# Another recorded order of steps and other engine choices for the first part of an attention and Fourier-mixing kernel

## The chip, the cores and the metric

The kernel runs on one core of a Trainium2 chip. A core has TensorE (PE, matrix products, 128x128 cells that can also work as smaller tiles), VectorE (DVE), ScalarE (ACT) and GpSimd (POOL), each with its own instruction queue that is worked off in order, and SyncE (SP), from whose queue nearly all DMAs of this kernel are issued. The metric is the device time of one execution in microseconds (us).

## The reference

Everything is float32; the two weights of the last step come as float64. 8 batches, 8 heads, a sequence of 576, heads of 64.

```
attention, for each batch and head, q and k scaled by 64**-0.25:
  phi(t) = exp(h - max(h)) / sqrt(128),  h = t @ omega.T - sum(t*t)/2      # 128 features
  kv = phi(k).T @ v;  z = sum of phi(k) over the sequence
  out = (phi(q) @ kv) / (phi(q) @ z + 1e-6)
x = heads side by side                       # (8, 576, 512)
u  = x + real(fft over features(fft over sequence(x)))
un = (u - mean(u)) / sqrt(var(u) + 1e-6)
result = u + relu(un @ w_ch1) @ w_ch2        # w_ch1 512x2048, w_ch2 2048x512
```

## The kernel before, in words

The program has two parts. Both are written as streams: Python generators that yield a `Step` ahead of each small group of instructions. A step names the engine (or a choice of engines with a cost for each), what it waits for, which buffers and PSUM banks it takes and gives back, and, for TensorE, the tile mode. `Listing.run` (L194) goes through the streams, decides whose step comes next and, where there is a choice, on which engine, and so writes each engine's queue. What runs when on the chip is then set by these queues and by semaphores.

**First part** (to about 422 us). Lanes `pairs(0)`, `pairs(1)`, `pairs(2)` go through 32 pairs of heads; `attn(n)` (L585) is one pair:

- `loads` brings k (L388) and q (L391), `load_v` v (L396); TensorE transposes (L524, identity as the other operand) and `evicted` copies the result out as kqT on VectorE (L538) or ScalarE (L540).
- Features: L618 in 64x128 tiles for the first six pairs and 64x64 tiles after; VectorE takes the maximum (L561), ScalarE the exponential (L578).
- kv: L652 in 64x64 tiles, copied out at L666 (VectorE) or L668 (ScalarE). Exponentials of q are transposed by L524 again and copied to qeT.
- Numerator and denominator: L699 and L707 in 128x64 tiles; reciprocal on VectorE (L716, L717), quotient on VectorE (L728) or ScalarE (L724).

`mix(b)` (L740) is the Fourier step of a batch: folds (L755, L757, L761, L771, L784) on VectorE or GpSimd, products with tables of cosines and sines (L811 in whole 128x128 tiles and L821), copies (L834), a second set of products (L861, L872), sums, and stores of u. At the very start `warm` (L495) has six matmuls on zeros that depend on no load, and `first` (L503) transposes omega (tile om).

Woven in: `narrow` (L439) turns float64 weights into float32 in several passes, the first on ScalarE (L451) or GpSimd (L449), the others on VectorE, the last sum (L467) on either; `w2_parts` (L1273) and `weight_sums` (L1352) form sums of weight blocks; and four blocks of 128 tokens go through both layers of the MLP plainly (`plain_of`: L1127 with relu at L1111 on VectorE or L1113 on ScalarE, then L1150). Each float32 matmul stands in the profile as two records.

In this part the choices are recorded in the string `PICKS`, one character for each step. Its value, divided by 36, gives the position of the stream in the list of those that wait, as remainder, and `other` as quotient: 0 takes the engine that by the planner's clock would be done first, 1 the next. `FIRST` holds the constants of that clock; `turn` is what a change of tile mode costs TensorE in it; VectorE and GpSimd share one time `PORT`, up to which operations on the shared port wait in the plan.

**Second part** (from about 422 us). The other 3584 tokens go through the MLP in seven blocks of 512, by a scheme of Strassen's kind with fewer products and more sums. L1454 and L1596 are first-layer products, L1839 second-layer ones; sums are made by `add` (L1414, recorded as L1419) on VectorE or GpSimd, the result of products by L1477, L1497, L1401 (VectorE), L1479, L1511, L1577, L1812 (ScalarE) and others. `wash` (L1944) clears three PSUM banks behind a GpSimd memset (L1948). `w1_sums` (L1653) builds sums of weight blocks into tiles so5, so6 and so3, `w1_inner` (L1681) sums within them into tile rx. Here nothing is recorded: the planner decides on the go, with the clock `SECOND`, from the state in which the first part leaves its engines:

```
    listing.run([wash(), late_turns(), late_norms(), halves(), load_leaves(), token_sums(0), w1_sums(), w1_inner()])
```

Of the kernel before, what the change touches and what calls it, by code (L numbers as in the profile page):

```python
# [32 lines left out]
NL = 2  # L33
# [3 lines left out]
PE, ACT, DVE, POOL, SP, NONE = "pe", "act", "dve", "pool", "sp", "none"  # L37

PORT = "port"

class Clock(NamedTuple):
# [11 lines left out]
    270.0, 0.036, 0.2, 0.12, {PE: 0.163, ACT: 0.105, DVE: 0.085, POOL: 0.02}, {DVE: 0.12, ACT: 0.055},  # L53
# [3 lines left out]
SLACK, AHEAD = 0.3, 4.0  # L57
# [3 lines left out]
DIGITS = "0123456789abcdefghijklmnopqrstuvwxyzABCDEFGHIJKLMNOPQRSTUVWXYZ!#$%&()*+,"  # L61
# [6 lines left out]
    "40e0f03eafdaegebg3NbcbeefdcOdeccfgdb37ghj0gjj7hlP79Kj7ik97i8S7efhjffeHldfPiehdjfdOShgihidaKOdbRhciff"  # L68
    "ecgOfeejdfdPdeeedgSfdffdOfd8Kiii88jhd8jP8b99i8e8jcddghjgheiifcecdciieicgPgdef9cdghbkededfgchbggb79ij"
    "8hi7hjaPN97aj9gfffeg8eif8hcej1jccc7ehidbhffLiQObfbeG766gggfcbjahj9Ofghhjj8dgkkgT6jghff8de6dUjfhbgegh"  # L70
    "MefRafjUf8jgciSjeckkhjakkaeikggjlioklnRSgodonON7l7l6nnj9icadc97cibPJIej788a7edhclhkmjjagVijihkkfpVim"
    "oklilTTillaghlhnmVjkmpjkhhnmkimlgglmbjpjjg9d9alafhhdjlacdTback0j766k7lh4g89Gck6gkki77gij5ijhgj6dimni"
    "3ndjgi6Kc4jldlaikbkaijbhf75dcjlmUVUDGci45jciekajkkUk5kihoUeaeobaiodlenMSdonbiiljjcWjjkboijjkkhgMfkik"
    "hiflkmOFF99nol5m8jT7naabda89Rbj97ecdl8cjilegiPkQb4acahg57ebbgabgdjkdTkk6eceebb5f9dg4RGce486ggg6egfhh"
    "fg4g9egf5cbdRgfhhhcgjhggejigibbmHnbedijj6Neb7biihi9bgihckaffPa8cijdhbdghbaeibdefffacjiciQSfi9JJ75ih5"
    "jgjI699ajfg6g7fgefd65bO6Kalkkgd5jgjikagfldliPJpeoaeeOPQNejadgilgicljiSSFe65k56kl5Hk7j67S9lilk9gliih6"
    "ffUgec4fg4dbgg7fedaif5gfbheefilddddddeQhg9kbfncggRcfkkafkag6ngb65p5Hopoj4bhoaXbelli68bjjl5b7dlhiQRhi"
    "lflhpkgiWomjknmmmUimnjbjhnJjkm5akPFgedccff6Wf7idUVhi8Th3fogbqp8fgmkeidjna7ckeXYghmnmffnjeo79q6547oa4"
    "nlkpd7aceonnc8bViVicilbhmjim8fh7Snn8l5mkkPjgfRhfhihg8ghfbS4kjf83j4lllb79jei8mnUblfnmmiolpilOki9Mh5l5"
    "pmnaOm79jjVmkbblekFiji9a9kffjgjikhiihfgjafhgfigh4g50fff0ba5fdh9dghda77hgfdcbg8eO988jcehefibjjkellPcc"  # L80
    "fcdhgcihPgcffba2f82b3c98cbcdcd6a299efgddb9KGQQbefLa9ecf74gg9867RgP9idg8kgOhePP7be6ff2e5cc8fbMgdaf8f8"
    "9hd9bM999bddc7cdb7ec9effegd7ibhgeQ8hKf7ccghRlUikh7m5lWmm5dkMQ6M71fS6d1gdb99747ifddh8fdhhdhfdbihgiljn"
    "gWgijgQ93ekal8kEhIIbT3jjagkb9k9eTfhkhlje34m49974i666h68fa7e6eHK79982975a894a39M8cM8b4aK7ab984fgO8ebc"
    "J8b86ce8Pb5fc9cbe6caff3a9b94f8dIQe9abd876e9fdcFPdb7ffbf99SS8RiLa4a7gPbajfgg8gdfhg2i2787Hf6OcdIN5d3LH"
    "accd46ddeaa72d9c7bbaa4bb9a9bc7c0777dghhdP7Bfddebd76ff1fddIe9949438686bcGaca8F348dHc67a5be95Hb55d15E4"
    "9Gc1F5a9a6844634458E584E59189970955888574443113301110"
# [39 lines left out]
class Listing:  # L126
# [4 lines left out]
    def __init__(self, buffers):  # L131
        self.clock = FIRST
        self.free = dict.fromkeys((PE, ACT, DVE, POOL, SP, NONE, PORT), 0.0) | self.clock.begin
        self.buffers = {name: [0.0] * n for name, n in buffers.items()}
        self.made = {}
        self.moved = 0.0
        self.mode = "whole"
        self.banks = [0.0] * 8
        self.got = None
        self.front = 0.0  # L140
# [15 lines left out]
    def start(self, step, ready, before, other=False, due=None):  # L156
# [35 lines left out]
        return t + (clock.turn if eng == PE and step.mode != self.mode else 0.0), eng  # L192

    def run(self, streams, picks=None):  # L194
# [16 lines left out]
        for g in streams:  # L211
            due, g = g if isinstance(g, tuple) else (0.0, g)
            go_on([due, g, None, (0.0, 0.0), NONE])
        while todo:
            pick = next(picks, None)
            other, n = divmod(DIGITS.index(pick), 36) if pick else (0, 0)
# [11 lines left out]
            step = item[2]  # L228
# [64 lines left out]
def kernel(  # L293
# [291 lines left out]
    def attn(n):  # L585
# [18 lines left out]
        def pairs_of(js, *ts):  # L604
# [3 lines left out]
                (0.25 if wide else 0.23) * len(js),  # L608
# [52 lines left out]
        def keep():  # L661
# [23 lines left out]
            1.22,  # L685
# [54 lines left out]
    def mix(b):  # L740
# [102 lines left out]
        for c in range(NC3):  # L843
# [3 lines left out]
                1.38 if c < NL else 0.94,  # L847
# [425 lines left out]
    def w2_parts():  # L1273
# [22 lines left out]
        for i, made_of in (  # L1296
# [16 lines left out]
            yield Step(SP, 3.0, 4.0, after=(("w2t", i),), kb=7 * 256, makes=("w2l", i))  # L1313
# [696 lines left out]
```

## Time and profile before

| | |
|---|---|
| median of three executions | 1138.2 us (1138.0 to 1138.83) |
| profiled execution, its own time | 1138.29 us |
| its span | 1136.3 us |
| TensorE busy | 1116.1 us (98%) |
| VectorE busy | 871.9 us (77%) |
| ScalarE busy | 544.6 us (48%) |
| GpSimd busy | 423.5 us (37%) |
| DMA moved | 258.28 MB |
| granted TensorE clock, mean | 0.999 |

An engine's busy time is the sum of its instructions' spans; where it is near the span, the engine is either at work or called so by a model (ends of matmuls are modelled, so starts are the firmer times). The chain that ended last is followed back from the last instruction and tells what it hung on. Windows show how the shares differ in time: the first part is a mixture of all engines, the second mostly products. A wait is idle time just before an instruction, and the arrow behind it names who ended it. L numbers are lines of the kernel.

### The profile page before, as it was taken

The page shows a single profiled execution, that of the slowest core. Times are in us where ns is not written, and L with a number is a line of the kernel's source. Part 1 is how long each engine was busy: PE and PEld are TensorE (multiplying, and loading weights), DVE is VectorE, ACT ScalarE, POOL GpSimd, SP SyncE. Part 2 cuts the span into 40 slices and gives each one's busy share as a digit, 9 for nine tenths or more (in the row PEclk, how much of TensorE's full clock was granted, in tenths as well). Part 3 has the DMA queues.
Part 4 walks back from the last instruction along what each step waited for, and adds up shares of the span by engine and source line. Part 5 has one row for each costly group of instructions (what it writes and reads, how often), then busy time and mean ns, then how long its engine had stood idle before and what let it go on. Part 6 is the DMA issues. An engine that isn't in the chain of part 4 may idle for free.

```text
span 1136.3 us, 34262 instructions
## 1 busy us (share of the span) xinstructions
PE 1116.1 (98%) x13639; PEld 1039.7 (91%) x13640; DVE 871.9 (77%) x1735; ACT 544.6 (48%) x1646; POOL 423.5 (37%) x435
## 2 busy tenths in 40 slices
PE   8999999999999999989999999999999999999998
PEld 7778888879868768989999999999999999999998
DVE  6999899987576646787777678678678678678666
ACT  7898898856535216724424424423523522522311
POOL 2443443553573124512711710720630540550361
PEclk9999999999999999999999999999999999999999
DMA  7856766575663238597797797798698798788576
GB/s 241 229 184 178 225 181 199 176 216 173 206 203 120 84 109 266 184 320 248 220 333 242 212 333 250 205 314 275 199 302 276 222 288 291 216 264 296 185 224 203
DMA packets 187965, 258.28 MB, mean 227 GB/s; under 512 B 52384, under 2 KB 83360, under 8 KB 187808
## 3 DMA queue, kind: packets, MB, share of 16 engines
q1 hardware_dynamic: 187312, 255.85, 72.2%
q8 instruction: 108, 1.77, 0.6%
q14 instruction: 49, 0.40, 0.1%
q10 hardware_dynamic: 496, 0.26, 0.1%
HBM read 212.27 MB, written 47.97 MB: 229 GB/s over the span
## 4 chain that ended last, share of the span: by engine, by line
PE 92%; DVE 2%; DMA 2%; ACT 2%; issue 1%; SPq 0%; POOL 0%; DVEq 0%; POOLq 0%
PE banks L1839 31%; PE banks L1454 27%; PE banks L618 5%; PE banks L1127 5%; PE banks L524 5%; PE banks L1150 4%; PE banks L1596 4%; PE banks L652 3%; PE banks L699 2%; PE banks L861 2%; PE banks L811 1%; DMA kq<-in_q_dram 1%; PE banks L821 1%; PE banks L872 1%; ACT e L578 1%
## 5 line engine op out<-in xcount | busy, mean ns | idle before, releaser
L1839 PE MATMUL banks<-wl,sums 128*128 128x128 f32 x1792 | 219.0, 275 | 3.3 <-issue 3.2
L1839 PEld LDWEIGHTS banks<-wl,sums 128*128 128x128 f32 x1792 | 209.3, 192 | 3.7 <-issue 3.7
L578 ACT ACTIVATE e<-banks,nmx 128x128 f32<-128x128 f32 x576 | 163.9, 421 | 23.0 <-DVE nmx L561 22.5
L1419 POOL TENSOR_TENSOR hid<-hid 128x512 f32<-128x512 f32 x98 | 128.8, 1318 | 118.7 <-ACT hid L1511 66.5
L1839 PE MATMUL banks<-wl,hid 128*128 128x128 f32 x1344 | 170.4, 275 | 0.4 <-DVE part L1817 0.4
L1839 PEld LDWEIGHTS banks<-wl,hid 128*128 128x128 f32 x1344 | 160.1, 192 | 0.6 <-DVE part L1817 0.6
L561 DVE TENSOR_REDUCE nmx<-banks 128x8 f32<-128x1024 f32 (+1 forms) x96 | 89.3, 951 | 18.8 <-PE banks L618 14.6
L1454 PE MATMUL banks<-rx,wx 128*128 128x128 f32 x672 | 88.8, 275 | 0.0
L1812 ACT ACTIVATE s<-banks 128x128 f32<-128x128 f32 x112 | 31.0, 277 | 109.4 <-PE banks L1839 89.1
L1497 DVE TENSOR_TENSOR hid<-banks,s 128x512 f32<-128x512 f32 x72 | 49.8, 691 | 42.9 <-PE banks L1454 35.6
L1454 PEld LDWEIGHTS banks<-rx,wx 128*128 128x128 f32 x672 | 81.8, 192 | 0.0
L618 PE MATMUL banks<-om,kqT 64*64 64x128 f32 (+1 forms) x2088 | 79.0, 275 | 1.3 <-ACT kv L668 0.7
L618 PEld LDWEIGHTS banks<-om,kqT 64*64 64x64 f32 (+1 forms) x2088 | 64.5, 138 | 12.3 <-issue 3.4
L1817 DVE TENSOR_TENSOR part<-banks,s 128x128 f32<-128x128 f32 x112 | 32.2, 289 | 48.6 <-PE banks L1839 47.0
L1127 PE MATMUL banks<-unT,w 128*128 128x128 f32 x512 | 65.4, 279 | 1.7 <-DVE qeT L538 1.7
L467 POOL TENSOR_TENSOR w<-w,raw 128x512 f32<-128x512 f32 x28 | 37.5, 1349 | 78.5 <-DVE raw L461 78.5
L1479 ACT ACTIVATE s<-banks 128x512 f32<-128x512 f32 x65 | 38.7, 595 | 57.4 <-PE banks L1454 56.9
L1127 PEld LDWEIGHTS banks<-unT,w 128*128 128x128 f32 x512 | 60.2, 192 | 4.4 <-issue 2.3
L1401 DVE CUSTOM_DVE_ANT_0 hid<-banks,s 128x512 f32<-128x512 f32 x63 | 43.6, 692 | 27.0 <-PE banks L1454 24.7
L1477 DVE TENSOR_TENSOR s<-banks,hid 128x512 f32<-128x512 f32 x70 | 48.4, 692 | 19.7 <-PE banks L1454 17.5
L1855 ACT ACTIVATE banks<-banks 128x128 f32<-128x128 f32 x56 | 14.7, 262 | 96.5 <-PE banks L1839 93.9
L1419 DVE TENSOR_TENSOR hid<-hid 128x512 f32<-128x512 f32 x90 | 57.5, 683 | 4.5 <-ACT hid L1550 4.5
(195 smaller groups left out, 2399.0 us busy)
## 6 DMA issues: line engine op xcount, KB each, us to landing
wl<-w2l SPq DMA_DIRECT2D x392, 256.0 KB
wx<-w1l SPq DMA_DIRECT2D x126, 256.0 KB
raw<-in_moe_w_ch_dram SPq DMA_DIRECT2D x32, 512.0 KB
kq<-in_k_dram SPq DMA_DIRECT2D x32, 288.0 KB
kq<-in_q_dram SPq DMA_DIRECT2D x32, 288.0 KB
vd<-in_v_dram SPq DMA_DIRECT2D x32, 288.0 KB
u<-us SPq DMA_DIRECT2D x36, 256.0 KB
ur<-us SPq DMA_DIRECT2D x36, 256.0 KB
```

The lines of the kernel that those rows point to most:

```text
L524: nc.tensor.transpose(ps[:, (j - j0) * 128 : (j - j0 + 1) * 128], src(j), ident[:])
L561: nc.vector.tensor_reduce(nmx[:, :, 0:num], pps[:, :, 0 : MF * num].rearrange("p b (c m) -> p b c m", m=MF), axis=AX.X, op=ALU.max, negate ...
L578: nc.scalar.activation(out=e[:, c + (i if num == 1 else 0), :], in_=pps[:, i, MF * c : MF * c + MF], func=AF.Exp, bias=nmx[:, i, c : c + 1],)
L618: nc.tensor.matmul(pps[cols, c, MF * m : MF * m + MF], lhsT=kqT[rows, j, cols], rhs=om2[rows, :],)
L1127: nc.tensor.matmul(hp[:, 0:TP], lhsT=w1[:, dc, 128 * fc : 128 * fc + 128], rhs=unTs[key][:, dc, :], start=(dc == 0), stop=(dc == NDC - 1),)
L1150: nc.tensor.matmul(yp[:, 0:DM], lhsT=hs[fc][:, 128 * i : 128 * i + 128], rhs=w2[:, fc, :], start=(fc == 0), stop=(fc == NFC - 1),)
L1419: eng.tensor_tensor(out=o, in0=l, in1=r, op=op)
L1454: nc.tensor.matmul(ps[:, P * f : P * f + P].rearrange("f (b q) -> f b q", q=Q), lhsT=left[:, P * f : P * f + P], rhs=right, start=start an ...
L1477: nc.vector.tensor_tensor(out=s[:], in0=ps, in1=cell_of(addend, f, t), op=ALU.add)
L1497: nc.vector.tensor_tensor(out=o, in0=ps, in1=kept[saved][:], op=ALU.add)
L1596: nc.tensor.matmul(cell.rearrange("f t (b q) -> f t b q", q=Q), lhsT=w[:, d, col : col + 128], rhs=right[:, :, d].rearrange("f (t b) q -> ...
L1839: nc.tensor.matmul(ps[:, 0:128], lhsT=left[:, f], rhs=wls[j, i, n][:, f], start=start and f == 0, stop=(f == 3), skip_group_check=True,)
```

## The change

- `PICKS` is a new string: another order of the same steps, and other choices of engine, for the whole first part.
- `other` now gives the position of the engine in the step's own list, not its rank by planned end. Without a recorded pick (the second part), it is None and the engine with the earliest planned end is taken as before.
- With recorded picks an operation on the shared port waits in the plan for single recorded stretches of the other engine (`unlocked`), not for one common time.
- Constants of the plan: `turn` 0.12 to 0.2 us; costs of L618, L699, L811 with L821, and L861 steps; the store of second-layer weights w2l counts as shorter and smaller.

The arithmetic and the number of matmuls stay as they are. Lines behind L230 move by up to 20. The rows of `PICKS` that follow the first are left out.

```diff
--- before.py
+++ after.py
@@ -50,7 +50,7 @@
 
 
 FIRST = Clock(
-    270.0, 0.036, 0.2, 0.12, {PE: 0.163, ACT: 0.105, DVE: 0.085, POOL: 0.02}, {DVE: 0.12, ACT: 0.055},
+    270.0, 0.036, 0.2, 0.2, {PE: 0.163, ACT: 0.105, DVE: 0.085, POOL: 0.02}, {DVE: 0.12, ACT: 0.055},
     (PE, SP, NONE), {SP: 0.72, ACT: 2.9, PE: 1.1},
 )
 SECOND = Clock(190.0, 0.15, 0.0, 0.1, {}, {}, (PE, ACT, DVE, POOL, SP, NONE), {})
@@ -65,25 +65,25 @@
 
 
 PICKS = (
-    "40e0f03eafdaegebg3NbcbeefdcOdeccfgdb37ghj0gjj7hlP79Kj7ik97i8S7efhjffeHldfPiehdjfdOShgihidaKOdbRhciff"
...
+    "10ffee0e41acfeaddc9debbbb43egf9iQgfcfiKafe9L9c0agg9i9ceheg8hijIPe6hdiii9icc87898idjiPefcacdifageeebK"
...
 )
 
 
@@ -131,6 +131,7 @@
     def __init__(self, buffers):
         self.clock = FIRST
         self.free = dict.fromkeys((PE, ACT, DVE, POOL, SP, NONE, PORT), 0.0) | self.clock.begin
+        self.locks = {DVE: [], POOL: []}
         self.buffers = {name: [0.0] * n for name, n in buffers.items()}
         self.made = {}
         self.moved = 0.0
@@ -153,7 +154,20 @@
                 best = key
         return best[3], best[0]
 
-    def start(self, step, ready, before, other=False, due=None):
+    def unlocked(self, eng, t):
+
+        locks = self.locks[POOL if eng == DVE else DVE][-16:]
+        changed = True
+        while changed:
+            changed = False
+            for begin, end in reversed(locks):
+                if end < t - 8:
+                    break
+                if begin <= t + 1e-9 and t < end - 1e-9:
+                    t, changed = end, True
+        return t
+
+    def start(self, step, ready, before, other=None, due=None):
 
         clock = self.clock
         queued = before in step.engines and len(step.engines) == 1
@@ -182,11 +196,16 @@
 
         def begin(e):
             u = ready[1] + clock.lag.get(e, 0.0) if before == PE and not queued else 0.0
-            return max(t, u, self.free[e] if e != NONE else 0.0, self.free[PORT] if step.on_port(e) else 0.0)
-
-        engines = sorted(step.engines, key=lambda e: begin(e) + step.engines[e])
-        eng = engines[other and len(engines) > 1]
-        if due is not None and POOL in engines and due > self.front + AHEAD:
+            b = max(t, u, self.free[e] if e != NONE else 0.0)
+            if not step.on_port(e):
+                return b
+            return max(b, self.free[PORT]) if other is None else self.unlocked(e, b)
+
+        if other is None:
+            eng = min(step.engines, key=lambda e: begin(e) + step.engines[e])
+        else:
+            eng = tuple(step.engines)[other]
+        if due is not None and POOL in step.engines and due > self.front + AHEAD:
             eng = POOL
         t = begin(eng)
         return t + (clock.turn if eng == PE and step.mode != self.mode else 0.0), eng
@@ -213,7 +232,7 @@
             go_on([due, g, None, (0.0, 0.0), NONE])
         while todo:
             pick = next(picks, None)
-            other, n = divmod(DIGITS.index(pick), 36) if pick else (0, 0)
+            other, n = divmod(DIGITS.index(pick), 36) if pick else (None, 0)
             may = []
             for item in todo if pick is None else [todo[n]]:
                 got = self.start(*item[2:], other, None if picks_ else item[0] + item[2].bias)
@@ -234,6 +253,7 @@
                 self.front = max(self.front, item[0] + step.bias)
             if step.on_port(eng):
                 self.free[PORT] = end
+                self.locks[eng].append((begin, end))
             done = end + step.late + clock.tail.get(eng, 0.0) + (clock.hop if eng != NONE else 0.0)
             if step.kb:
                 self.moved = max(self.moved, end) + step.kb / clock.rate
@@ -605,7 +625,7 @@
 
             yield Step(
                 PE,
-                (0.25 if wide else 0.23) * len(js),
+                (0.222 if wide else 0.205) * len(js),
                 mode="rows" if wide else "quarters",
                 after=(("kqT", n, js[-1] // 4 * 4), "om2"),
                 take=("duo",),
@@ -682,7 +702,7 @@
         )
         yield Step(
             PE,
-            1.22,
+            1.165,
             mode="halves",
             after=(("kv", n), ("qeT", n, 0), ("qeT", n, 1), ("qeT", n, 5)),
             take=("duo",),
@@ -797,7 +817,7 @@
         for n, (tab, name) in enumerate(((cs, "cs"), (sn, "sn"))):
             yield Step(
                 PE,
-                1.9,
+                2.03,
                 after=(("fold", b, n), name),
                 take=("duo",) + (("y",) if n == 0 else ()),
                 give=("fold",) if n == 1 else (),
@@ -844,7 +864,7 @@
 
             yield Step(
                 PE,
-                1.38 if c < NL else 0.94,
+                1.46 if c < NL else 0.91,
                 mode="whole" if c < NL else "halves",
                 after=tuple(("y", b, n) for n in range(2)) + ("cd", "sd"),
                 take=("duo",),
@@ -1310,7 +1330,7 @@
                 yield from op(o, l, r, after=last, makes=("w2t", i) if o is t4 else None)
             last = (("w2l", i),)
 
-            yield Step(SP, 3.0, 4.0, after=(("w2t", i),), kb=7 * 256, makes=("w2l", i))
+            yield Step(SP, 0.4, 1.0, after=(("w2t", i),), kb=300, makes=("w2l", i))
             for n, t in ((0, c11), (1, c21), (4, c22)):
                 nc.sync.dma_start(w2l[i][n].rearrange("p (f m) -> p f m", f=4), t)
             for n, t in ((2, sums[0]), (5, sums[1])):
```

In the built program this comes to the following. In the first part TensorE changes its tile 229 times in place of 257, and enters a run of transposes L524 from other matmuls 84 times in place of 97. On VectorE, L755 goes 11 to 7, L784 22 to 14, L1292 10 to 16, L1111 20 to 32; on ScalarE, L451 24 to 14, L1113 44 to 32, L724 40 to 50; on GpSimd, L449 8 to 18, L755 5 to 9, L784 10 to 18, L1292 34 to 28. Omega's transpose (L503) stands ahead of `warm` on TensorE, where it stood behind the first four kq transposes. SP issues the second pair's k load ahead of the first v loads. Since the second part is planned from the state that the first leaves, some of its sums move too: of the `add` sums of the so tiles VectorE has one in place of nine and GpSimd fourteen in place of six.

More of the change, by code (lines that the diff above doesn't have):

```diff
@@ L67 @@
 PICKS = (
-    "40e0f03eafdaegebg3NbcbeefdcOdeccfgdb37ghj0gjj7hlP79Kj7ik97i8S7efhjffeHldfPiehdjfdOShgihidaKOdbRhciff"
[L69 to L86, printed above, removed]
+    "10ffee0e41acfeaddc9debbbb43egf9iQgfcfiKafe9L9c0agg9i9ceheg8hijIPe6hdiii9icc87898idjiPefcacdifageeebK"
+    "9gcMdjf8efba9fPjid9f9bfb9bjfhQjgjhIejehegh6hafjc6jjji8khif7dde9cdgfhcjhejgfdgh6kNhhidjbbLkfegebekdhd"
@@ new lines @@
+    "bhdf6g6gaccQcif15S8iifbcgibcdjcffdegic66acc6Nd9fdde8b8cIf7aha9clbLhjic7gKg7hcgfdccRehecihdigcddf7fJG"
+    "d7fjcciag78ihakfggLg7NkekdfliShQaej6ijddgkekOdh6ikdhhfJfj6Pdh6bGadi9eadfefPbh9gNhef8ahg7ebhkbalMhch9"
+    "f9eNdfheddhN7hNfdMefecg9eNchd0Nd9cSbFccj9Tafl58eeg8iilOd5ckfe67jeelc789jl7fh78g9RijejgH8h79Fd4ekfb5a"
+    "8Sbke9lMkhk6g6jc6dagh97Lgddkidgiff3e8dfg47ccH7bjiedikic9dj97gbeficjGhgNceSI7iNfii9jhecb7hhhd9hghed9h"
+    "8bgTRhegfedhajfgadLabdegeQf7cffge5dG8ai64L8jecbNe5ddb9jhf7hgIgbicfe9hecb5eeacbdeafcgchi7c8jacjhgbjM4"
@@ new lines @@
+    "TjaeP4c88he9LTe6cfd9fhgMikT6cTdeedf7K889kQf9M8jjJijddab7kPbKhSSa7Gddi56fdc6c8dgdcbc68bc8f76R9daaafcc"
+    "e76gfN9dlca9ld9dcRdkI5d97oKkgdJnnn9afiklinjihd6mdh6hce7gddllLkf9cic7e98clf77c6Pgde9ai9PgdH78fRic49Rh"
+    "ceikfh5KgKf9ge7dchb6h79d4847f9idcdegijdklmabgdgbSicejeff5Qj7c8bKkcch7bj7GdimghcmmllN9hlmdkm8filmlP8l"
+    "lnSh4mfcmhjeQjJdcihgigidbe6hjk7fcjgcgl6ffkeb9dd66iQL7b6d9hcidje8a536efkjecTf89e8ed8e4ngi7kThj7ikfJdT"
+    "cllhen5eQ8h95d9eeekmia7g7ghijchdglNSWkehlfm9ehad7gh4NhMce3fff3fb9ghg9d8ddQg8gg4h5gbg1fN78fe0bbj27Okk"
@@ new lines @@
+    "H5eiib6hc6bah8KiLb2dgbcfdikajjLfajgRiecagch5cccdg9bhdEO99hhdchNhgf9gcidbPdfffdgheg2MN7efadeffeHddQO7"
+    "9aNccdNgbcafNfKc6gOiiefJdd7cggQ2MIccb47ac7bad29NcJa5be8g5eb98G36bN8a8Ldg6eg689g5icaHecj6L6abdeM8d8JP"
+    "ffac78faMeeb6dIIQaeb76fbffPceacacL9b879eeKdJcbaM83M494945dadbabfdb8SJKhaMNcg4L6Rgb7eKhOfeb71fbbLh6Ph"
+    "8h88887JSb6hiQTjjghdadiih40a06kb95eia58ik66hg5S15ehdhba9kihjggb8eg9jag8Njfhgek8Khf19eajeji23gNGHd8L9"
+    "7cee2acbb42d98a0Kb33cc557689967dd5Nd38F8c6ecdbfPcd3fb63bfH7dcf6a58aH673c8eaK9LE5aa1aa833b5a7K9ab7J58"
@@ L87 @@
+    "b68HLba48a6c5ef5aabe3Eb57H240F43497862552bbbb8a26J68775224536777576335265430353157749664569766Faa186"
+    "858aabeeK62b776adJde14K6129a450AD6D60A46555CB12222100"
 )
```

## The prediction

> **What bounds the kernel now.** I read the page first. TensorE is busy almost throughout, and nine tenths of the chain that ended last are its own instructions.
>
> ```profile
> PE 1116.1 (98%) x13639; PEld 1039.7 (91%) x13640; DVE 871.9 (77%) x1735; ACT 544.6 (48%) x1646; POOL 423.5 (37%) x435
> PE 92%; DVE 2%; DMA 2%; ACT 2%; issue 1%; SPq 0%; POOL 0%; DVEq 0%; POOLq 0%
> ```
>
> The whole span hides two parts, so next the table by stretches of 25 us (columns after the stretch: its length, then TensorE, its weight loads, VectorE, ScalarE, GpSimd, with instructions in brackets):
>
> ```profile
> 0.00:25.00 25.00, 21.67 (x355) 18.97 (x355) 16.05 (x27) 17.85 (x61) 6.47 (x14) 1.00 0.83 255
> 25.00:50.00 25.00, 23.88 (x566) 20.47 (x566) 24.52 (x44) 23.36 (x90) 10.26 (x8) 1.00 0.84 216
> ...
> 75.00:100.00 25.00, 22.85 (x585) 18.52 (x583) 23.12 (x50) 23.06 (x85) 9.86 (x10) 1.00 0.71 209
> ...
> 150.00:175.00 25.00, 25.00 (x548) 22.46 (x538) 24.21 (x60) 22.63 (x82) 11.31 (x12) 1.00 0.66 198
> ...
> 250.00:275.00 25.00, 25.00 (x577) 21.66 (x576) 16.56 (x33) 17.09 (x65) 12.17 (x11) 1.00 0.54 161
> ```
>
> Up to 150 us TensorE has gaps, and VectorE is as full as TensorE (24.52 of 25 us); from 150 to 250 both are full; after 250 only TensorE is. So before about 132 us a shorter TensorE order needs a VectorE that keeps up. TensorE's waits (third view: what, for whom, total us, times, longest) come to 17.2 us in the first part when its idle time is summed; the named ones that matter:
>
> ```profile
> PE banks L524 <- DMA kq<-in_k_dram: 2.3, 1, 2.3
> PE banks L524 <- DMA kq<-in_q_dram: 2.1, 2, 1.4
> PE banks L699 <- issue: 1.7, 1, 1.7
> PE banks L1127 <- DVE qeT L538: 1.7, 1, 1.7
> ```
>
> **What a change of tile costs.** TensorE's timeline (start, busy us, source line, tile rows*columns, operand shape, count) gives it from the distance between starts:
>
> ```profile
> 155.69 0.33 PE L524 MATMUL banks<-ident,e 128*128 128x128 f32 x1
> 155.85 1.25 PE L811 MATMUL banks<-sn_sb,fold 128*128 128x160 f32 x8
> ...
> 157.78 1.10 PE L618 MATMUL banks<-om,kqT 64*64 64x128 f32 x32
> 158.70 1.23 PE L652 MATMUL banks<-vd,e 64*64 64x65 f32 x72
> ...
> 164.32 0.66 PE L524 MATMUL banks<-ident,e 128*128 128x128 f32 x4
> 164.91 1.15 PE L699 MATMUL banks<-kv,qeT 128*64 128x65 f32 x32
> ...
> 172.38 1.32 PE L618 MATMUL banks<-om,kqT 64*64 64x128 f32 x40
> 173.63 0.66 PE L524 MATMUL banks<-ident,e 128*128 128x128 f32 x4
> 174.12 0.27 PE L524 MATMUL banks<-ident,kq 128*128 128x128 f32 x1
> ```
>
> 32 records of L618 into L652, which has the same 64*64 tile, take 158.70 - 157.78 = 0.92, so 40 would take 1.15; the 40 before a 128*128 transpose take 1.25, 0.10 more. Four transposes before another transpose take 0.49, before L699's 128*64 tile 0.59: again 0.10 for leaving. One transpose behind L652 takes 0.16; the other three of a four take 0.33, 0.11 each, so the first transpose behind other work costs 0.05 more. A change of tile is thus 0.15 to 0.20 us (L707 into another tile reads 0.10 dearer as well).
>
> **Part 1, TensorE's order: -5.4 us.** In the order of the built kernel's instructions the first part has 229 changes of tile where it had 257, and 84 entries into a run of transposes where it had 97. 28 changes by 0.15 to 0.20 are 4.2 to 5.6; I take 4.7, the sum when each run of instructions is priced by its own form. 13 entries by 0.05 are 0.7. No matmul is added or removed. With these prices and no waits, from the first transpose to the last weight-sum matmul, the order needs 395.7 us in place of 401.1.
>
> **Part 2, the start: +3.3 us and -4.8 us.** The transpose of om (L503) moves ahead of the six warm-up matmuls L495, and it waits for om's DMA, issued at 0.72 and landed near 3.55 us. Queued behind it on TensorE are the warm-up's 12 records, 2.73 us from 1.03 to 3.76, which today lie under the first loads. The first kq transposes then start near 6.4, 2.7 later, and some run cold: 0.3 to 0.9, I take 0.6. Against that, SP issues the second pair's k load third, ahead of the first v loads, so it lands near 5.4 in place of 9.2: the 2.3 us wait at 6.7 us goes. The seventh pair's q load gets 13.9 us between issue and use in place of 5.1, the eleventh's is no longer behind a weight load: the 2.1 us of the two q waits go, and about 0.4 of smaller ones. That is 4.8. In VectorE's queue the same work is then done some 1.4 us earlier at 12.6 us.
>
> **Part 3, engine choices: +0.4 us.** With unchanged means per form, the first part's sums go: VectorE 388.7 to 386.9 us, ScalarE 423.8 to 414.5, GpSimd 177.3 to 200.5 (ten more L449 by 1.57, four more L755 by 2.36, eight more L784 by 1.02, less six L1292 by 1.33). Work on GpSimd hides under TensorE, whose cover is 25 us in 25. But it stretches VectorE's operations on SBUF: VectorE's first part holds 18.4 us above the shortest of each form beside 177.3 us of GpSimd, 0.10 for each us, so 23 us more stretch it by about 2.4. Two thirds of the part run with TensorE full and VectorE with room, and VectorE's own sum falls 1.8, so from 0 to 2.4 reaches the path; I take 0.4.
>
> The planner's constants (L618, L699, L811, L861, the w2l store) issue nothing themselves: zero. First part: -5.4 + 3.3 - 4.8 + 0.4 = -6.5. The bounds are -11 (the waits at L699 and L1127, 1.7 each, also go, and neither a cold start nor stretch costs anything) and -1 (VectorE holds up all before pair twelve, below).
>
> **Part 4, the seam: +4.2 us.** The second part is planned anew from the first one's end, and four so sums move from VectorE to GpSimd:
>
> ```profile
> 424.87 1.27 POOL L1419 TENSOR_TENSOR rx<-w,rx 128x512 f32<-128x512 f32 x1
> 427.70 0.69 DVE L1497 TENSOR_TENSOR hid<-banks,s 128x512 f32<-128x512 f32 x1 [5.48 <-DMA us<-uh]
> 428.43 1.64 ACT L1577 ACTIVATE banks<-hid 128x512 f32<-128x512 f32 x3 [1.08 <-DVE hid L1497]
> 429.08 1.99 PE L1596 MATMUL banks<-unT,w 128*128 128x256 f32 x8 [0.52 <-ACT banks L1577]
> 429.20 2.49 DVE L1419 TENSOR_TENSOR so<-w 128x512 f32<-128x512 f32 x4
> ```
>
> Today L1497 runs on VectorE at 427.70 and the so sums behind it. In the new program the four stand on GpSimd behind the last rx sum, 426.14 + 4 x 1.27 to 1.35 = 431.3; a fifth, which adds their result, stands on VectorE directly ahead of L1497 and waits for them: 0.68 more, 432.0. Behind it queue L1497, ScalarE's L1577 and TensorE's L1596, which so starts near 433.3 in place of 429.1. TensorE has nothing between. 432.0 - 427.7 is 4.3, of which I take 4.2; 3.5 if the first sums start a little sooner, 5.5 if VectorE stretches them as at 486 us (next view).
>
> **Part 5, the rest: 0 +- 1.5 us.** The second part's one long wait today is:
>
> ```profile
> 488.52 1.75 DVE L1888 TENSOR_TENSOR ur<-ur,part 128x512 f32<-128x512 f32 x1
> 490.19 0.68 DVE L1419 TENSOR_TENSOR sums<-hid,sums 128x512 f32<-128x512 f32 x1
> 490.94 1.19 PEld L1839 LDWEIGHTS banks<-wl,sums 128*128 128x128 f32 x10 [3.37 <-issue]
> ```
>
> The sum that TensorE waits for there moves to GpSimd behind two ur additions (1.7 each); after it come the last two, so the wait is again near 3.5.
>
> **Sum.** The profiled execution took 1138.29, 0.1 above the median of 1138.2. 1138.29 - 6.5 + 4.2 = 1136.0, or 1135.9 against the median. 0.2% is 2.3 us, about what a measurement of this kernel tells from no change: bounds 1135.9 and 1140.5.
>
> **Rivals.**
> *VectorE binds (slower).* Up to the twelfth pair, at 132.2 us today, TensorE needs 117.3 priced without waits and then 113.8, but VectorE's work needed by then is 102.5 and then 102.2: 0.3 less. If VectorE sets that stretch, the first part gains 0.3 there and 1.9 behind it, 2.2; the seam takes 4.2, and stretch by GpSimd 1.0: 1138.2 + 3.0 = 1141.2. It decides from the point where the first part gains less than 1.9. For: 24.52 of 25 us. Against: VectorE idles 9 us of the first 25, and at pairs two to nine its work needed falls by 2 to 5 us. The Trainium skill, "SBUF — State Buffer", section "SBUF: two separate sides", speaks for this rival: it says that VectorE and GpSimd share a port pair as an exclusive lock, the loser blocked for the whole instruction. The trace agrees at 486 to 490 us, where additions of 0.68 took 1.75; by it, a whole 2.4 of stretch in the full stretches would give 1142.6.
> *The waits fall further (faster).* The two 1.7 us waits and half the small ones (about 2) go as well, or the seam's wait is covered: -5 more, 1131. For: VectorE and ScalarE both have less to do. Against: an order has its own late operands, and the seam's queue leaves no way round.
> *Nothing is left (same).* New small waits eat the 2.3 that remain: 1138.
>
> **How the numbers follow.** Forecast 0.44 (its own range 1133.5 to 1138.5, a half of it faster by the bound), waits fall 0.25, VectorE 0.22, nothing left 0.09. Faster 0.22 + 0.25 = 0.47; same 0.20 + 0.09 = 0.29, slower 0.02 + 0.22 = 0.24. To hold eight in ten the range reaches over most of both rivals: 1129.5 to 1142.
>
> **What would show it.** In the new trace: TensorE's first kq transpose near 6.4 us and no k wait at 7; fewer transposes of 0.16 and exits of 0.10; the waits of the first part near 16 us; the first L1454 of the second part some 6.5 us earlier; GpSimd's four so sums in a row and behind them a TensorE gap of about 4.7 us at L1596; one wait near 3.5 us at L1839. It is wrong if VectorE is full with TensorE waiting on L538 or L561 between 25 and 132 us, or if L1596 does not wait.

## The result, and the profile after

The changed kernel takes 1174.7 us (median of 6 runs, 1172.0 to 1175.1) against 1138.1 us (6 runs); the ratio is 1.031, interval 1.030 to 1.033. It is 36 us slower, where 2 us faster had been forecast, and lies 33 us above the range.

The page first, the same two lines as before:

```profile
PE 1126.3 (96%) x13639; PEld 1045.7 (89%) x13640; DVE 890.4 (76%) x1727; ACT 539.3 (46%) x1629; POOL 482.4 (41%) x469
...
PE 79%; DVE 12%; ACT 3%; issue 3%; DMA 1%; POOL 1%; SPq 0%; DVEq 0%; POOLq 0%
```

The span grew by 36.4 us, VectorE's busy time by 18.5 and GpSimd's by 58.9. Of the chain that ended last VectorE now carries 12% (141 us), where it had 2%. In the new numbering, lines after L230 are up to 20 higher: L476 is the old L456, L481 the old L461, L487 the old L467, L775 the old L755, L1616 the old L1596.

Where the time lies is told by one instant, the first matmul of `wash`, which ends the first part: 422.5 us before, 453.8 after. From there to the end of the span it is 713.8 and 718.8. So 31.3 us were lost in the first part and 5.0 behind it.

The table by stretches, in the columns of before (length, TensorE, weight loads, VectorE, ScalarE, GpSimd, granted clock, share of the DMA engines, GB/s):

```profile
0.00:25.00 25.00, 19.81 (x330) 17.53 (x330) 13.37 (x22) 15.66 (x56) 5.70 (x14) 1.00 0.81 241
25.00:50.00 25.00, 24.70 (x528) 21.71 (x526) 24.21 (x41) 23.34 (x87) 10.13 (x7) 1.00 0.88 232
...
75.00:100.00 25.00, 20.77 (x503) 17.20 (x499) 23.32 (x45) 19.17 (x73) 17.08 (x19) 1.00 0.67 206
...
150.00:175.00 25.00, 20.65 (x453) 16.81 (x455) 24.27 (x33) 16.71 (x61) 18.64 (x16) 0.96 0.53 166
...
250.00:275.00 25.00, 22.64 (x298) 17.08 (x296) 22.53 (x50) 9.75 (x32) 14.53 (x15) 0.93 0.38 111
```

From 25 to 250 us VectorE is as full as it was, but TensorE is not: from 150 to 175 us it is busy for 20.65 us, where it had been busy for all 25. VectorE gets less done in the same time. Why this is so is seen in the groups of VectorE's operations in the first part. The lines give operation, operands, shapes, count, busy time in us, mean in ns and idle time. Two passes over the weights, in the kernel before:

```profile
L456 DVE SCALAR_TENSOR_TENSOR w<-w,sign 128x512 uint32<-128x512 uint32 x32 | 22.8, 712 | 0.3
L461 DVE SCALAR_TENSOR_TENSOR raw<-raw,sign 128x512 f32<-128x512 uint32 x32 | 22.0, 686 | 0.6
```

and in the changed one:

```profile
L476 DVE SCALAR_TENSOR_TENSOR w<-w,sign 128x512 uint32<-128x512 uint32 x32 | 30.7, 958 | 1.5 <-DVE sign L474 0.5
L481 DVE SCALAR_TENSOR_TENSOR raw<-raw,sign 128x512 f32<-128x512 uint32 x32 | 30.6, 955 | 0.5
```

The same 32 instructions of the same shape take a third longer. One of them in the timeline:

```profile
55.17 2.37 POOL L775 TENSOR_TENSOR half<-x 128x1024 f32<-128x1024 f32 x1 [4.83 <-DVE mid L811]
56.07 2.02 DVE L481 SCALAR_TENSOR_TENSOR raw<-raw,sign 128x512 f32<-128x512 uint32 x1
58.01 0.41 DVE L581 TENSOR_REDUCE nmx<-banks 128x2 f32<-128x256 f32 x1
```

GpSimd's addition runs from 55.17 to 57.54. VectorE's L481 starts at 56.07 and ends at 58.09, 0.55 after GpSimd's end, though 0.69 is what it takes alone. It has stood for the rest of the other's instruction. That is what the Trainium skill, "SBUF — State Buffer", section "SBUF: two separate sides", says of the port pair that the two share: an exclusive lock, the later one blocked. The trace agrees. The two lines together hold 64 instructions: the 34 that had no GpSimd instruction beside them took 685 (L476) and 688 ns (L481) in the mean and none over 700; the 26 beside a GpSimd addition took 1176 and 1513.

To sum this up over the first part I take, for every VectorE instruction, the time above the fastest twentieth of its own line and access pattern (where it is over 0.05 us) and call it stretch. It is 9.8 us before and 45.2 after; 32 of the 45 lie between 25 and 250 us, where VectorE has no room. By GpSimd's instruction beside it, most lies with L467 (11.6, before 0.3) and L755 (11.4, before none), in the old numbering. Counts of instructions moved VectorE's sum by -1.8 us, as reckoned; the means moved it by +34.6. GpSimd's instructions grew too: longer means added 16 us to its work in the first part.

### The profile page after: what moved, and what is told of

Its sections match the earlier page's. It is cut to its first block, busy times and chain, and to the rows that moved or that the text cites. A ratio compares the mean times of both kernels' runs of the same rounds, so it can differ in the third digit from the quotient of the medians.

```text
span 1172.7 us, 34241 instructions
## 1 busy us (share of the span) xinstructions
PE 1126.3 (96%) x13639; PEld 1045.7 (89%) x13640; DVE 890.4 (76%) x1727; ACT 539.3 (46%) x1629; POOL 482.4 (41%) x469
## 4 chain that ended last, share of the span: by engine, by line
PE 79%; DVE 12%; ACT 3%; issue 3%; DMA 1%; POOL 1%; SPq 0%; DVEq 0%; POOLq 0%
PE banks L1859 30%; PE banks L1474 26%; PE banks L1170 4%; PE banks L1616 4%; PE banks L1147 4%; ACT e L598 3%; PE banks L544 3%; DVE nmx L581 2%; PE banks L638 2%; DVE w L476 2%; PE banks L672 2%; PE banks L719 1%; DVE sign L474 1%; PE banks L881 1%; DVE raw L481 1%
## 5 line engine op out<-in xcount | busy, mean ns | idle before, releaser
L598 ACT ACTIVATE e<-banks,nmx 128x128 f32<-128x128 f32 x576 | 163.5, 423 | 50.1 <-DVE nmx L581 49.5
L1439 POOL TENSOR_TENSOR hid<-hid 128x512 f32<-128x512 f32 x96 | 125.4, 1310 | 118.7 <-ACT hid L1531 69.2
L581 DVE TENSOR_REDUCE nmx<-banks 128x8 f32<-128x1024 f32 (+1 forms) x96 | 88.6, 949 | 18.2 <-PE banks L638 17.9
L1147 PE MATMUL banks<-unT,w 128*128 128x128 f32 x512 | 64.2, 277 | 1.0 <-ACT e L598 1.0
L1439 DVE TENSOR_TENSOR hid<-hid 128x512 f32<-128x512 f32 x92 | 60.8, 708 | 5.4 <-ACT hid L1570 5.4
L487 POOL TENSOR_TENSOR w<-w,raw 128x512 f32<-128x512 f32 x27 | 36.7, 1361 | 63.7 <-DVE raw L481 55.6
L1474 PE MATMUL banks<-unT,w 128*128 128x128 f32 x464 | 60.2, 275 | 0.0
```

The costliest lines, as they stand in the source:

```text
L581: nc.vector.tensor_reduce(nmx[:, :, 0:num], pps[:, :, 0 : MF * num].rearrange("p b (c m) -> p b c m", m=MF), axis=AX.X, op=ALU.max, negate ...
L598: nc.scalar.activation(out=e[:, c + (i if num == 1 else 0), :], in_=pps[:, i, MF * c : MF * c + MF], func=AF.Exp, bias=nmx[:, i, c : c + 1],)
L1147: nc.tensor.matmul(hp[:, 0:TP], lhsT=w1[:, dc, 128 * fc : 128 * fc + 128], rhs=unTs[key][:, dc, :], start=(dc == 0), stop=(dc == NDC - 1),)
L1439: eng.tensor_tensor(out=o, in0=l, in1=r, op=op)
L1474: nc.tensor.matmul(ps[:, P * f : P * f + P].rearrange("f (b q) -> f b q", q=Q), lhsT=left[:, P * f : P * f + P], rhs=right, start=start an ...
```

## The experiments

The ratios are against runs of the kernel before on the same chip, whose median lay between 1138.1 and 1139.4 us. "First part" is the start of `wash` in the profiled run. Theory A: the port, by the new order's laying GpSimd beside VectorE. B: only the larger amount of work on GpSimd. C: TensorE's order has late operands by itself. D: GpSimd's results come late.

| run | median us | ratio to before (interval) | first part us |
|---|---|---|---|
| before | 1138.1 | | 422.5 |
| after | 1174.7 | 1.031 (1.030 to 1.033) | 453.8 |
| a_thin | 1150.4 | 1.010 (1.006 to 1.014) | 429.3 |
| b_thin | 1147.2 | 1.007 (1.003 to 1.011) | 429.0 |
| b_thin2 | 1136.9 | 0.998 (0.997 to 1.000) | 419.6 |
| a_449act | 1174.4 | 1.031 (1.024 to 1.039) | 451.4 |
| b_449pool | 1144.2 | 1.005 (1.002 to 1.007) | 423.6 |
| a_seam | 1177.1 | 1.034 (1.031 to 1.037) | 452.1 |
| a_start | 1176.1 | 1.033 (1.030 to 1.036) | 453.1 |
| a_thin_seam_start | 1145.8 | 1.006 (1.004 to 1.008) | 422.0 |
| a_memset | 1159.6 | 1.018 (1.015 to 1.021) | 435.6 |
| a_dvethin | 1162.0 | 1.020 (1.017 to 1.023) | 438.5 |
| b_dvethin | 1138.1 | 0.998 (0.997 to 1.000) | 419.5 |
| a_467dve | 1181.0 | 1.037 (1.034 to 1.039) | 461.0 |
| b_k1 | 1137.0 | 0.999 (0.997 to 1.000) | 418.8 |
| b_k1_ur | 1141.0 | 1.002 (1.001 to 1.003) | 419.7 |

### GpSimd's operations cut short: a_thin, and the controls b_thin and b_thin2

```diff
-        eng.tensor_tensor(out=dst, in0=dst, in1=lof, op=ALU.add)       # and five like it
+        thin(eng, out=dst, in0=dst, in1=lof, op=ALU.add)               # on GpSimd: first eighth of the width
...
-        if step.eng == POOL:                                           # L449; not in b_thin2
+        if False:
```

So that the parts left out are defined, the tiles half and fold are one lasting buffer each, cleared once by GpSimd at the start.

> The changed kernel with GpSimd's large operations of the first part cut to an eighth of their width (L467, L755, L771, L784, L922, L923 in the old numbering) and L449 moved to ScalarE; order and VectorE's work as before, part of GpSimd's sums left out. Theory A (the lost 36 us are VectorE's operations held up by GpSimd's on the shared SBUF port, because the new order lays them beside each other while VectorE is full): the first part gets 20 to 30 us shorter, about 1146 to 1154 us. Theory B (only the 23 us more of work on GpSimd): the same here. Theory C (TensorE's new order has late operands by itself, the longer VectorE operations do not matter): within 5 us of 1174.

> The same cut in the kernel before, as the control. Theory A: VectorE's first part holds only 9.8 us of stretch there, some 5 of it where VectorE is full, so 1131 to 1138 us. Theory C: 1138. If it falls by 20 us or more, the cut itself does something else and the run of the changed kernel proves nothing.

> The control again, the kernel before with the same cut but L449 left where it was. In b_thin ScalarE's moved L449 held up its exponentials between 25 and 50 us (TensorE there 20.2 of 25 us). If that was all: 1131 to 1138, no slower than the kernel before. If it stays near 1147, the cut itself slows the kernel before.

a_thin gave back 24.3 us, all of it in the first part, where VectorE's stretch fell to 4.4 us. The same two passes there:

```profile
L493 DVE SCALAR_TENSOR_TENSOR raw<-raw,sign 128x512 f32<-128x512 uint32 x32 | 22.1, 691 | 0.6
L488 DVE SCALAR_TENSOR_TENSOR w<-w,sign 128x512 uint32<-128x512 uint32 x32 | 22.0, 687 | 5.9 <-ACT w L483 5.1
```

The first control missed: b_thin got slower by 8 us. In it L449, moved to ScalarE, waited there for a weight's DMA with the exponentials queued behind it:

```profile
ACT w L463 <- DMA raw<-in_moe_w_ch_dram: 5.1, 1, 5.1
...
25.00:50.00 25.00, 20.23 (x357) 17.47 (x355) 16.97 (x31) 17.15 (x63) 1.16 (x3) 0.86 0.70 171
```

With L449 left in place (b_thin2) the cut takes 1.6 us from the kernel before, and 2.9 from its first part. a_thin moves L449 too, so its like is b_thin: there the first part got 6.5 us longer, here 24.6 shorter. What the move alone costs in the new order was not measured by itself; in a_thin VectorE waits 5.1 us for it (the second line above). By either control the cut is worth far more in the new order than in the old. C falls: at 1150 most of the loss was gone, with TensorE's order unchanged.

### Only the amount: a_449act and b_449pool

```diff
-        if step.eng == POOL:                                           # a_449act
+        if False:
...
-        if step.eng == POOL:                                           # b_449pool
+        if step.eng == POOL or i in (2, 6, 7, 8, 9, 10, 14, 18, 22, 26):
```

> The changed kernel with all 18 L449 on ScalarE (L451), so that GpSimd's first part falls below that of the kernel before plus ten. Theory B (amount): about 1143 us, as the kernel before with the seam. Theory A (alignment): only the 3.6 us of stretch beside L449 and some of what follows goes, 1163 to 1172. Theory C: 1174.

> The kernel before with ten more L449 on GpSimd (18, as many as in the changed kernel), order unchanged: 15.7 us more work on the port. Theory B (amount): 15.7/23 of 31 us, so about 1159. Theory A: the order before keeps the others apart, only these ten can collide, at most one 0.6 us VectorE pass each: 1139 to 1146. Theory C: 1138 to 1140.

Taking 30 us of GpSimd's work away changed nothing that these two runs can tell from 1174 (2.4 us in the first part of the profiled run; stretch 40.5 in place of 45.2). This misses A's 1163 to 1172 as well as B's 1143, and the run is not clean: the moved L449 make VectorE wait 4.5 us for ScalarE, which can hide a gain of about that size, but hardly one of 31. The firmer run is the other. Adding 16.6 us to the old order cost 5 us, 1.1 of it in the first part of the profiled run, and its stretch rose from 9.8 to 13.2 only. The median is 1144.2, where B expected 1159. B falls as the main cause. What the new order has changed is which operations run beside each other.

### Busy but not reading: a_memset

```diff
+            eng.tensor_tensor(out=part(out), in0=part(in0), in1=part(in1), op=op)   # an eighth
...
+            while left > 0:
+                nc.gpsimd.memset(w1s[:, 0, 0 : min(left, 512)], 0.0)
+                left -= 512
...
             eng.tensor_tensor(out=out, in0=in0, in1=in1, op=op)                     # an eighth: the result
```

> The changed kernel with GpSimd's large operations cut to an eighth again, but each followed by GpSimd memsets (which read nothing) of about the time that the cut took away, then one more narrow piece that gives the result: GpSimd is as busy and its results as late as in the changed kernel, only it does not read SBUF meanwhile. Theory A (the shared port): VectorE's operations stay short, 1150 to 1158 us. Theory D (GpSimd's results come late, or its queue is too full; the cut kernels were faster for that): 1168 or more.

The memsets stand from 23 to 248 us, the time in which VectorE is full. GpSimd was busy from 75 to 100 us for 21.9 us, more than in the changed kernel (17.1), and VectorE's two passes still ran at their own pace:

```profile
75.00:100.00 25.00, 23.61 (x591) 19.23 (x589) 22.93 (x48) 21.23 (x83) 21.90 (x60) 1.00 0.80 239
...
L503 DVE SCALAR_TENSOR_TENSOR raw<-raw,sign 128x512 f32<-128x512 uint32 x32 | 22.5, 703 | 0.5
L498 DVE SCALAR_TENSOR_TENSOR w<-w,sign 128x512 uint32<-128x512 uint32 x32 | 22.2, 693 | 1.5 <-POOL w L472 0.5
```

The first part was 18.2 us shorter than in the changed kernel, the time 1159.6: 2 us above what A expected and 8 under D's 1168. Of the stretch left (13.1) 5.9 lies beside memsets, most of the rest beside L449, L1292 and the narrow pieces.

### Room on VectorE: a_dvethin, b_dvethin

```diff
-            bits, bits, 3, sign[:], op0=ALU.logical_shift_left, op1=ALU.bitwise_or
+            bits[:, 0:64], bits[:, 0:64], 3, sign[:, 0:64], op0=ALU.logical_shift_left, op1=ALU.bitwise_or
...
-        nc.vector.tensor_scalar(sign[:], bits, 0xFF800000, None, op0=ALU.bitwise_and)
+        nc.vector.tensor_scalar(sign[:, 0:64], bits[:, 0:64], 0xFF800000, None, op0=ALU.bitwise_and)
```

> The changed kernel with two of VectorE's passes over the weights (L456 and L459 in the old numbering) cut to an eighth of their width, about 44 us of VectorE's 417 in the first part; GpSimd as it is. If VectorE being full is what hands the stretch on to TensorE: 25 to 35 us faster, 1140 to 1150. Theory D: within 8 us of 1174.

> The same two passes cut in the kernel before, as the control, some 33 us of VectorE's 386. TensorE waits there 17.5 us in all after the start, a part for DMAs: 3 to 9 us faster, 1129 to 1136. If it gains as much as the changed kernel does, fullness of VectorE was no difference between the two.

The changed kernel gained 12.7 us (15.3 in its first part), the kernel before 1 (3.0). So room on VectorE is worth far more in the new order than in the old, which is the way by which stretch reaches TensorE, but the gain was half of what was expected. One line, first in the changed kernel and then in the control, says why:

```profile
L476 DVE SCALAR_TENSOR_TENSOR w<-w,sign 128x64 uint32<-128x64 uint32 x32 | 15.1, 473 | 1.5 <-DVE sign L474 0.5
...
L456 DVE SCALAR_TENSOR_TENSOR w<-w,sign 128x64 uint32<-128x64 uint32 x32 | 8.4, 263 | 0.4 <-ACT w L451 0.2
```

An eighth of the width still took 473 ns in the mean, where the same instructions took 263 ns in the control, in the old order. An instruction that waits for the port waits as long when it is short: the 17 of this line beside a GpSimd addition took 0.49 us more than those beside nothing at full width (1176 and 685 ns), and 0.48 more at an eighth (697 and 220). The stretch stayed at 44.7 us, and the cut took 24 us from VectorE (30.7 to 15.1, and 19.8 to 11.1 for the other pass), not 44.

### Work taken from GpSimd to VectorE: a_467dve

```diff
-        eng = nc.gpsimd if step.eng == POOL else nc.vector
-        eng.tensor_tensor(out=dst, in0=dst, in1=lof, op=ALU.add)
+        nc.vector.tensor_tensor(out=dst, in0=dst, in1=lof, op=ALU.add)
```

> The changed kernel with all 27 L467 (the last sum of a narrowed weight, the line beside which VectorE lost most) on VectorE: GpSimd loses 36.7 us of work, VectorE gains 27 sums of 0.68, 18.4 us, and loses the 11.6 us of stretch beside them. If the port and VectorE's fullness explain the first part: VectorE is 5 to 7 us longer in sum, 1174 to 1182 us. If a good part of the loss is that GpSimd's queue is late (Theory D): 1155 to 1165.

1181.0: GpSimd relieved of 36.7 us, and the kernel 6 us slower, as VectorE's sum says. D falls as the main cause. It has one visible instance in the changed kernel: SP's queue stood 15.5 us for an addition on GpSimd, a k load waited behind it, and TensorE waited for the load at 274 us.

```profile
SPq L957 <- POOL x L943: 15.5, 1, 15.5
...
PE banks L544 <- DMA kq<-in_k_dram: 3.6, 1, 3.6
```

### The seam and the start: a_seam, a_start, and all three

```diff
-    *(part(w, d, f) for w in (outer_weights(i), l, r)), op, (POOL, DVE), makes=("sum", i, d, f),
+    *(part(w, d, f) for w in (outer_weights(i), l, r)), op, (DVE,) if i in (5, 6) else (POOL, DVE), makes=("sum", i, d, f),
...
+        for _ in range(6):                                              # a_start: moved here from warm()
+            nc.tensor.matmul(omps[:, 0:128], lhsT=ur1[:, 0:128], rhs=ur1[:, 0:128])
         nc.tensor.transpose(omps[:, 0:128], om2d, ident[:])
```

> The changed kernel with the sums into so5 and so6 bound to VectorE. The prediction's seam (four sums on GpSimd, then one on VectorE ahead of L1497): the wait of 5.5 us at L1596 (L1616 in the new numbering) goes down to under 1 and the kernel is 4 to 5 us faster, about 1170. Rival (the seam's wait is only moved to the next sums or to the second layer): 1174.

> The changed kernel with the six warm-up matmuls ahead of omega's transpose again. The new trace has the first kq transposes at 6.65 us and TensorE at half its pace until 11. If VectorE, which is full from then on, starts its first maxima as much earlier: 3 to 5 us faster, 1169 to 1171. Rival (the loads of the first pairs set the start anyway): 0 to 1 us faster.

> The three together (GpSimd's large operations cut as in a_thin, but L449 left on GpSimd at full width; so sums on VectorE; warm-up first). If the causes are the port, the seam and the start, each by itself: 1150 - 5 - 4 + 1 to 3 for L449 = 1141 to 1144, within 4 us of the kernel before. If they overlap (the start hidden by VectorE, or L449 matters): 1146 or more.

The changed kernel's seam in the timeline, as the prediction had spelled it:

```profile
457.45 4.93 POOL L1439 TENSOR_TENSOR so<-w 128x512 f32<-128x512 f32 x4
...
462.42 1.73 DVE L1439 TENSOR_TENSOR so<-so,w 128x512 f32<-128x512 f32 x1 [8.79 <-POOL so L1439]
464.07 1.27 DVE L1517 TENSOR_TENSOR hid<-banks,s 128x512 f32<-128x512 f32 x2
464.78 1.64 ACT L1597 ACTIVATE banks<-hid 128x512 f32<-128x512 f32 x3 [6.09 <-DVE hid L1517]
465.44 3.06 PEld L1616 LDWEIGHTS banks<-unT,w 128*128 128x128 f32 x8 [5.72 <-ACT banks L1597]
465.44 3.78 PE L1616 MATMUL banks<-unT,w 128*128 128x256 f32 x8 [5.54 <-ACT banks L1597]
```

a_seam is a miss. The wait became 2.4 us in place of 5.5, not under 1: the four sums on VectorE now overlap GpSimd's rx sums and take 5.72 us (1.43 each). And since everything behind is planned anew, other operands were late at the second layer's first products. TensorE's waits between 440 and 560 us in a_seam:

```profile
PE banks L1859 <- ACT banks L1875: 2.8, 1, 2.8
PE banks L1616 <- ACT banks L1597: 2.4, 1, 2.4
PE banks L1859 <- ACT s L1832: 1.2, 1, 1.2
```

a_start is a miss too. TensorE did 22.36 us in the first 25 in place of 19.81, its first kq transposes stood 1.7 us earlier, those of the twelfth to the 17th pair 2.0, those of the 18th only 1.0, and the first part ended 0.7 earlier. Between the 17th and the 18th lies a lower granted clock (150 to 175 us: 0.90, where it had been 0.96), and over the whole first part the clock is 0.981 in place of 0.989, which can cost 3.4 us. So these two traces do not show that VectorE swallowed the earlier start: the clock can account for as much. (The expectation's half pace until 11 us was misread: only the nine first transposes, to 8.7 us, ran so.) a_thin_seam_start, with most of the collisions gone, has its first part at 422.0, 7.3 below a_thin and level with the kernel before. It differs from a_thin by the start and by L449, which is back on GpSimd; of the 7.3, 2.1 stand at the first kq transpose, and the rest, built up later, was not divided between the two. Its median of 1145.8 stays above the expected 1141 to 1144: in the second part TensorE waits 2.5 and 2.7 us at the same two places as in a_seam.

### Can the kernel before be bettered? b_k1, b_k1_ur

```diff
             nc.sync.dma_start(kq[:, R : 2 * R, :], q[b, h].rearrange(rows, r=R))
+            if n == 0:                                                  # the second pair's k, ahead of the v loads
+                kq = ld.tile([P, 2 * R, D], F32, name="kq", tag="kq")
+                nc.sync.dma_start(kq[:, 0:R, :], k[0, 2:4].rearrange(rows, r=R))
...
-            step = Step({POOL: 1.35, DVE: 0.7}, port=True, **kw, bias=15.0)          # b_k1_ur
+            step = Step({POOL: 1.35} if j == 0 else {POOL: 1.35, DVE: 0.7}, port=True, **kw, bias=15.0)
```

> The kernel before with the second pair's k load issued third on SP, ahead of the first two v loads, as in the changed kernel. The wait of 2.3 us at 6.7 us goes. If the first pairs are bound by it: 1 to 2.5 us faster, 1136 to 1137. If VectorE, full from 25 us on, hides it (as the start of the changed kernel's was): within 0.5 us.

> The kernel before with the second pair's k load issued third, and in the first block of the second part L1888's additions on GpSimd only, so that VectorE has one 1.75 us operation less ahead of the sum for which TensorE waits 3.2 us at 488 us. If that wait falls to 1.5 or less and no clock window is lost to it: 1133 to 1136 us, 0.2 to 0.5% faster than the kernel before. If the next operand of the second layer is late instead: 1137, as without the edit.

b_k1 takes the 2.3 us wait away and its first part is 3.7 us shorter in the profiled run; over 12 runs it is 2.1 us faster, with an interval that just reaches 1 (0.9971 to 1.0001). That is the best found here, and not firmly better. b_k1_ur is a miss: the wait at 488 us fell from 3.2 to 2.1, a new one of 2.5 us stood at 513 us, and the time rose by 0.2% (1.0006 to 1.0030).

## Why the prediction was wrong

**The step that failed is part 3, "engine choices: +0.4 us".** It took stretch as a rate, 0.10 us for each us of GpSimd, and multiplied it by 23 more us: 0 to 2.4, and 0.4 of it on the path. In this kernel stretch is no rate of the amount. It is set by which operations stand beside each other. By the prediction's own rule (time above the shortest of each form) it went from 18.4 to 51.7 us, by the stricter one above from 9.8 to 45.2: 33 to 35 us more, not 2.4. The second half of the step failed too. The prediction kept most of the stretch off the path because "two thirds of the part run with TensorE full and VectorE with room", but by its own table both engines are full from 150 to 250 us, so VectorE had room under a full TensorE only from 250 on, 172 us of 422. In the changed kernel VectorE was busy for 240 of the 250 us from 25 to 275, and for 23.0 of 25 from 300 to 325. On the chip the term is at least about 18 us of the first part's 31: a_memset gave back 18.2, with 13.1 of stretch left. a_thin gives 22, its 24.6 less the 2.9 that the cut is worth in the old order, though its L449 on ScalarE has a price of its own. a_thin_seam_start, without that move, gives 31.9, of which the same 2.9 and some 2 for the start go off: about 27. The runs do not divide it more finely.

The diff showed this, and I read past it. The old plan kept one `PORT` time, behind which every operation on the port had to start, so its order had them apart; `unlocked` in the new plan holds an operation back only where a recorded stretch of the other engine covers its start, and lets one that begins earlier run into it. That the new order's collisions come from this rule is argued from the code and not shown: a new search with the other rule was not tried. That the collisions cost the time is shown.

**The rival "VectorE binds"** had the mechanism, and the sentence on the lock. Its 1141 was 33 us short, because it priced VectorE's work with the means of before (102.2 us up to pair twelve), in which there is next to no stretch. The row that it should have used was in the prediction: additions of about 0.7 that took 1.75.

**Part 1, TensorE's order, -5.4: right.** The new trace has 229 changes of tile where the old has 257. From the first kq transpose to `wash`, TensorE takes 398.5 us before and 393.2 in a_thin_seam_start (1.7 of it for a clock of 0.996), 5.3 less, when waits over 0.2 us are taken off (a wait being what the distance between the starts of two neighbouring matmuls has above the shortest twentieth of such pairs). In the changed kernel it is 398.5 again; some 5 us of it are lost to a lower granted clock (0.96, 0.97, 0.93 and 0.93 in four stretches of 25 us).

**Part 2, the start: its places right, its sum worth nothing here.** The first kq transpose is at 6.65 us (6.4 foretold), the 2.3 us wait at 7 is gone, and so are the q waits. But TensorE's idle time in the first part went from 12.4 to 35.9 us, not down (the rows of the prediction's whole table sum to 12.4; its 17.2 is not in them): the named waits gave way to many others, most of them for VectorE or for ScalarE, which itself waited 49.5 us for VectorE's maxima (L581, the old L561), where it had been 22.5. In a_start a start 1.7 us earlier brought nothing in the time; how much of that is VectorE and how much the clock stays open.

**Part 4, the seam, +4.2: right, 0.8 short.** The wait at L1616 is 5.5 us where it was 0.5; the fifth sum took 1.73 in place of 0.68. **Part 5, 0 +- 1.5: a miss by a little.** Behind the seam TensorE's one named wait is 0.9 us where it was 3.2, so 2.3 better. That the part from `wash` to the end is 5.0 longer all the same goes with the granted clock after the seam's wait, 0.86 here:

```profile
450.00:475.00 25.00, 18.46 (x95) 15.09 (x95) 3.62 (x4) 7.71 (x14) 21.65 (x18) 0.86 0.69 209
```

This can cost up to 3.5. The three together (5.0, -2.3 and 3.5) make 6.2, 1.2 more than was measured.

## What to carry to other kernels

Where VectorE is full, price its instructions on SBUF by whether GpSimd will be reading SBUF beside them, one by one; the mean duration in an old order does not carry over to a new one, and cutting such an instruction short does not shorten its wait. When a recorded order is exchanged, compare what its planner forbade with what the new one allows before counting instructions. And a saving on TensorE, however sure (5 us here), is worth only what the engine that feeds it leaves open.

## What the runs showed of the hardware that was not expected

GpSimd's memsets, which read nothing, left VectorE's passes with two SBUF operands alone: the 16 of a_memset that ran beside one took 685 ns in the mean and none over 695, while in the changed kernel, beside GpSimd's additions, the same passes came to 958 and 955 in the mean of all 32. The two passes with one operand (L454 and L459) did feel the memsets: in a_memset they took 503 and 584 ns beside one (9 and 4 instructions), 413 and 427 with no GpSimd instruction beside them.

A wait of TensorE can cost more than its length. In the kernel before and in b_k1 the same wait of 3.2 us stands at the second layer; the windows around it read

```profile
475.00:500.00 25.00, 21.65 (x192) 21.33 (x191) 21.90 (x35) 6.22 (x21) 7.45 (x7) 1.00 1.05 332
```

in the one and

```profile
475.00:500.00 25.00, 21.79 (x184) 21.63 (x183) 20.95 (x37) 5.91 (x21) 5.48 (x5) 0.93 1.03 318
```

in the other: a granted clock of 0.93 over 25 us, 1.75 us of full pace lost, in one run and not in the other (behind the same wait 0.93 in b_thin2, 0.86 in b_dvethin and b_449pool). The Trainium skill, "TensorE: Matmul & The Clock Gate", section "Part 1: The HAM clock gate (the "warmup" mystery)", tells of windows of about 3.4 us that run freely and give half the clock after an idle one; by estimate, 0.93 and 0.86 are one and two such windows in 25 us. That far the trace agrees. But a wait shorter than a window should then leave the clock alone, and b_k1_ur has 0.93 behind a wait of 2.1 us:

```profile
475.00:500.00 25.00, 22.67 (x186) 22.34 (x186) 20.72 (x36) 5.94 (x20) 6.23 (x6) 0.93 1.02 329
```

Why the same wait has a slow window behind it in one run and none in another stays open. It may be a part of why b_k1's first part gained 3.7 us and its median 2.1.
